# Last tile's layer-2 rows transposed on TensorE, the w1 jobs' normalised rows loaded behind the last w2 loads, and three VectorE costs in the planner

## The chip, the cores and the metric

The kernel runs on one core of a Trainium2 chip. The metric is device time in microseconds (us) of one execution, the median of three runs. The core's engines run side by side, each through a list of instructions fixed when the kernel is built: TensorE (PE, with its weight loads shown apart as PEld), VectorE (DVE), ScalarE (ACT), GpSimd (POOL) and SyncE (SP). In this kernel SP and POOL mostly issue DMA transfers; the profile shows the issuing of a transfer as SPq or ACTq.

## The reference

The reference is the forward and backward pass of four residual layers over x, 2048 rows of 448 in bf16: a convolution layer A, a dense layer B, then A and B again with the same weights.

```python
def _A_ref(q, k, v, shift_k, ssm_k, ssm_D):    # q is the normalised x
    k_shift = ...                              # 4-tap shift of k along the sequence
    kv = k_shift * v
    y = irfft(rfft(kv, 2S) * rfft(ssm_k, 2S))[:S] + kv * ssm_D
    return q * y

def _B_ref(x, w1, w2):                         # w1 448x1792, w2 1792x448
    return silu(x @ w1) @ w2

x = A_q
x = x + _A_ref(_layernorm(x), A_k, A_v, A_shift_k, A_ssm_k, A_ssm_D)
x = x + _B_ref(_layernorm(x), B_w1, B_w2)
x = x + _A_ref(_layernorm(x), A_k, A_v, A_shift_k, A_ssm_k, A_ssm_D)
x = x + _B_ref(_layernorm(x), B_w1, B_w2)
```

It returns x and the gradients of all eight inputs for a given `grad_out`; those of w1 and w2 are sums over all 2048 rows and over both dense layers.

## The kernel before

The kernel has four stages. `Head` computes the convolution y through FFTs written as matmuls. `Flow.tile(j)` then takes the 16 tiles of 128 rows through both dense layers forward and back, software-pipelined over the tiles. `Tail` ends with the gradient of the convolution (`fft`, in 14 chunks of 1024 columns, then `loads` and `ends`) and with the weight gradients (`jobs("w2")`, `jobs("w1")`).

No order is written out. Every piece of work is an operation `s.op(cost, fn, r, w, prio, ...)`: the cost in us on each engine that may take it, the tiles it reads and writes, and a priority (lower is more urgent, mostly a due time). `Sched.plan` (from L257) plays these through with the given costs and with rates for the transfers, and fixes from that on which engine each runs and in which order; `Sched.emit` writes the instructions out in that order. On the chip an engine follows its list, and an instruction starts when the data and buffers that it needs are there. The argument `after=` ties an operation to others in the plan, and `behind=` says that it may be planned only when the others have been issued; neither is itself a wait on the chip. A cost is thus never executed: it moves work only through the plan.

What the change and the steps of the prediction touch:

- `ON_PE` (L595) lists the (tile, kind) pairs whose rows are transposed by four TensorE matmuls (`ps_t`, L645) and a copy out of PSUM (`nT`). All others are transposed by two DMA transposes on SP (`nT`, L636 and L637). Kind 0 is the first dense layer's input, 1 the second's, 2 the backward pass of the first. `Flow.turn` does this.
- The second dense layer of tile j: its normalised rows `n3` go through `turn` to the matmuls `ps_h` (L663), and ScalarE makes `aT` and `dT` from them (L700). The stores of these rows are DMA transposes into `turned` (L717) followed by `A_d<-turned` (L718); `GH_d<-ghT` (L711) stores the backward rows.
- For the last tile a part of `aT` is also transposed into `lastA` (L792). The gradient rows `gmov` (four transfers, L1087) are planned behind it.
- `jobs(which)` makes 7 jobs of 256 weight columns each. A job has two groups of 2 x 16 matmuls `ps_d` (L1169) of 128x448, which read a block `jb` of stored rows, 1 MB, and the matching other operand: for w2 `gmov` with the rows A1 and `G2` (`G` in the profile) with the rows A0; for w1 `nmov`, the normalised rows of the second layer with GH1 and of the first layer with GH0. `bring` loads the blocks on SP: plain copies `jb<-A_d` for w2 (L1114), DMA transposes `jb<-GH_d` for w1 (L1112). The blocks share three buffers, and for w1 a fourth, so a load waits until the block three places earlier is used up. `k.load` chains these loads by `behind=`.
- Before the change the first w2 block is planned behind the last tile's second DMA transpose (`self.last_rows`), and the four `nmov` loads (L1095, two for each of the layers, 896 KB each) are planned by priority alone.
- The chunks (`Tail.chunk`): two matmuls `ps_s` (L904) make the transform, a copy takes it to `xx_c`, two VectorE copies swap its halves (L912, L913), two VectorE products make `pq` (L918), 16 matmuls each turn these into `ps_v` (L924, L925), and copies take them to `B1k` and `Zg`. The copies out of PSUM can go to ScalarE or VectorE, as the planner sees fit. `ps_s`, `ps_v`, `ps_gkv` and `ps_gK` share three PSUM buffers.
- After the chunks come `ps_gkv` (L980), `ps_gK` (L1002), `ps_gD` (L1014) and `ps_sk` (L1051). The planner spreads the w2 jobs' matmuls between all of these as fillers.

Of the kernel before, what the change touches and what calls it, by code (L numbers as in the profile page):

```python
# [14 lines left out]
ACT = mybir.ActivationFunctionType  # L15
ALU = mybir.AluOpType
# [4 lines left out]
P = 128  # L21
# [68 lines left out]
def _copy(nc, eng, out, in_):  # L90
    if eng is nc.scalar:
        nc.scalar.copy(out, in_)  # L92
    else:
        eng.tensor_copy(out, in_)  # L94
# [38 lines left out]
class Sched:  # L133
# [26 lines left out]
    def at(self, base, *key):  # L160
        return base + NUDGE.get(key, 0.0)
# [188 lines left out]
def _pm(ap2d):  # L350
    return ap2d.rearrange("(p j) d -> p j d", j=J)
# [240 lines left out]
NT1 = {1: "nTG", 2: "nT3", 3: "nT3"}  # L592
COPIED = (0, 2,)
RAW = ("GH0", "GH1")
ON_PE = ((0, 0), (0, 1), (1, 0), (2, 0), (3, 0), (4, 0), (14, 2), (15, 0), (15, 2))  # L595


class Flow:
# [162 lines left out]
    def tile(self, j):  # L761
        nc, s, k = self.nc, self.s, self.k
        b = T_ * j
        at = lambda kind, base: s.at(base, j, kind)
# [11 lines left out]
        s.op({"POOL": 0.6}, lambda e: nc.gpsimd.dma_start(out=_pm(k.N_d[0][:])[:, j, :], in_=n1[:]), r=[n1], w=[k.st_[("n", 0, j)]], prio=b + 10, dma=("plain", 115e3))  # L776
        a1, s1 = self.silu(self.turn(n1, at("t1", b - 3), NT1.get(j, "nT1"), (j, 0) in ON_PE), 0, at("h1", b), (j, 0) in TURNED, j in COPIED)
        self.store(a1, "A0", j, b + 4)
# [7 lines left out]
        c = b + T_ + SKEW[0]  # L786
        a2, s2 = self.silu(self.turn(n3, at("t3", c + 2.7), "nT3", (j, 1) in ON_PE), 1, at("h2", c + 5.6), (j, 1) not in TURNED)
        up2 = self.last_up
        k.load = [] if (j, 1) in ON_PE else [self.last_rows]
        if j == NT - 1:  # L790
            k.lastA = s.vb("J", "lastA", [P, 4, P], BF16, "lastA")
            k.lastA_op = s.op({"SP": 1.2}, lambda e: nc.sync.dma_start_transpose(out=k.lastA[:], in_=a2[:, 0:4, :].rearrange("p a s -> p (a s)")), r=[a2], w=[k.lastA], prio=c + 10, dma=("turn", 131e3))  # L792
# [19 lines left out]
        d = c + T_ + SKEW[1]  # L812
        gh1 = self.grad_up(self.turn(G2, at("tG", d + 14), "nTG", (j, 2) in ON_PE), s1, at("gG", d + 16.9))
        self.store(gh1, "GH0", j, d + 20)
# [24 lines left out]
class Tail:  # L839
# [53 lines left out]
    def chunk(self, ci, Z, z, pr):  # L893
        nc, s, k = self.nc, self.s, self.k
        lo = 1024 * ci
        sp = self.sp[ci % 3]
        for i, nm in enumerate(("KV", "K")):
            s.op({"POOL": 0.6}, lambda e, i=i, nm=nm: nc.gpsimd.dma_start(out=sp[i][:], in_=k.SPEC_d[nm][:, lo:lo + 1024]), r=[k.spd[nm, ci // 2]], w=[sp[i]], prio=pr - 20, after=self.s1 if ci < 3 else (), dma=("plain", 262e3))
        ps = self.unit([P, 1024], name="ps_s2")

        def mm(e):
            zf = Z[:].rearrange("q a b -> q (a b)")
            for h in range(2):
                nc.tensor.matmul(ps[:, 512 * h:512 * h + 512], lhsT=k.Gsb[:, G_FWD, :], rhs=zf[:, lo + 512 * h:lo + 512 * h + 512], start=True, stop=True)  # L904

        o = s.op({"PE": 0.44}, mm, r=[z], w=[ps], prio=pr, after=[o for x in self.xx[ci % 3][1:] for o in x.readers])
        self.marks.append(o)
        xx, xa, xh = self.xx[ci % 3]
        s.op({"ACT": 1.02, "DVE": 1.15}, lambda e: _copy(nc, e, xa[:], ps[:]), r=[ps], w=[xa], prio=pr)

        def swap(e):
            nc.vector.tensor_copy(xh[0:64, :], xa[64:128, :])  # L912
            nc.vector.tensor_copy(xh[64:128, :], xa[0:64, :])  # L913

        s.op({"DVE": 0.75}, swap, r=[xa], w=[xh], prio=pr)
        for i, (B1, cnd) in enumerate(((self.B1k, True), (z, False))):
            pq = s.vb("P1", "pq", [P, 2, 1024], BF16, "pq")
            s.op({"DVE": 1.15}, lambda e, i=i, pq=pq: nc.vector.tensor_tensor(out=pq[:], in0=xx(), in1=sp[i][:].unsqueeze(1).to_broadcast([P, 2, 1024]), op=ALU.mult),  # L918
                 r=[xa, xh, sp[i]], w=[pq], prio=pr)
            pv = self.unit([P, 8, P], name="ps_v")  # L920

            def inv(e, pq=pq, pv=pv):
                for m in range(8):
                    nc.tensor.matmul(pv[:, m, :], lhsT=pq[:, 0, m * P:(m + 1) * P], rhs=k.Gsb[:, G_IAC, :], start=True, stop=False)  # L924
                    nc.tensor.matmul(pv[:, m, :], lhsT=pq[:, 1, m * P:(m + 1) * P], rhs=k.Gsb[:, G_IBC, :], start=False, stop=True)  # L925

            s.op({"PE": 0.92}, inv, r=[pq], w=[pv], prio=pr)

            def out(e, pv=pv, B1=B1, cnd=cnd):
                if cnd:  # L930
                    _copy(nc, e, B1[:, :, 32 * ci:32 * ci + 32].rearrange("p q (dh ds) -> p dh q ds", ds=4), pv[:].rearrange("p dh (q ds) -> p dh q ds", ds=4))
                else:
                    _copy(nc, e, Z[:, 8 * ci:8 * ci + 8, :].rearrange("p a b -> p (a b)"), pv[:].rearrange("p a b -> p (a b)"))

            s.op({"ACT": 1.03, "DVE": 1.17}, out, r=[pv], w=[B1], prio=pr)

    def loads(self, pr):
        nc, s, k = self.nc, self.s, self.k
# [143 lines left out]
    def jobs(self, which, pr):  # L1082
        nc, s, k = self.nc, self.s, self.k
        if which == "w2":
            gm = s.vb("res", "W1", [P, NT, D], BF16, "gmov")
            gs = [gm.sub() for _ in range(4)]
            gl = [lambda i=i: s.op({"SP": 0.4}, lambda e: nc.sync.dma_start(out=gm[:, 4 * i:4 * i + 4, :], in_=_pm(k.grad_out[0])[:, 4 * i:4 * i + 4, :]), w=[gs[i]], prio=pr - 30, dma=("plain", 458e3), behind=[k.lastA_op]) for i in range(4)]  # L1087
            groups = [("A1", [gs[t // 4] for t in range(NT)], lambda t: gm[:, t, :]), ("A0", k.G2v, lambda t: k.G2[:, t, :])]
        else:
            nm = [s.vb("PF", ("A1", "B1v")[i], [P, NT, D], BF16, "nmov") for i in range(2)]  # L1090
            nh = [[v.sub() for _ in range(2)] for v in nm]
            for i in (1, 0):
                for h in range(2):
                    hs = slice(8 * h, 8 * h + 8)
                    s.op({"SP": 0.4}, lambda e, i=i, hs=hs: nc.sync.dma_start(out=nm[i][:, hs, :], in_=_pm(k.N_d[i][:])[:, hs, :]),  # L1095
                         r=[k.st_[("n", i, j)] for j in range(8 * h, 8 * h + 8)], w=[nh[i][h]], after=self.done[i], prio=pr - 30 if i else pr + 0.5, dma=("plain", 917e3))
            groups = [("GH1", [nh[1][t // 8] for t in range(NT)], lambda t: nm[1][:, t, :]), ("GH0", [nh[0][t // 8] for t in range(NT)], lambda t: nm[0][:, t, :])]
        out7 = k.outs[7].rearrange("(c p) f -> p c f", p=DC)
        prev = []
# [2 lines left out]
        def fetch(p, gi, spare=False):  # L1102
            if (p, gi) not in have:
                have[p, gi] = (s.vb(*(("PF", "Minv") if spare else ("J", "jb")), [P, NT, 256], BF16, "jb"), [None] * NT, spare)
            return have[p, gi]

        def bring(p, gi, lo, hi, at=None):
            b, part, spare = fetch(p, gi, which == "w1" and (2 * p + gi) % 4 == 0)
            nm = groups[gi][0]
            src, n, fs = k.rows_d[nm], hi - lo, slice(256 * p, 256 * p + 256)  # L1110
            if nm in RAW:
                cost, kind, get = 0.3 * n, "load", lambda e: nc.sync.dma_start_transpose(out=b[:, lo:hi, :], in_=src[fs, P * lo:P * hi])  # L1112
            else:
                cost, kind, get = 0.4, "plain", lambda e: nc.sync.dma_start(out=b[:, lo:hi, :], in_=src[:, lo:hi, fs])  # L1114
            v = b.sub()
            part[lo:hi] = [v] * (hi - lo)
            k.load = [s.op({"SP": cost}, get,
                 r=[k.st_[(nm, j)] for j in range(lo, hi)], w=[v], prio=pr + 12.5 * p + gi if at is None else at, dma=(kind, 65e3 * n), behind=k.load, after=self.done[0] if spare else ())]

        if which == "w2":  # L1120
            bring(0, 1, 0, 16)
            for x in gl:
                x()
            for a in ((0, 0, 0, 15), (1, 1, 0, 16), (1, 0, 0, 15)):
                bring(*a)
        else:
            for p, gi, at in ((0, 0, pr), (1, 0, pr + 0.2), (0, 1, pr + 1), (1, 1, pr + 2)):
                bring(p, gi, 0, 16, at)
# [243 lines left out]
```

## Time and profile before

| what | value |
|---|---|
| median of 3 runs | 708.87 us (708.34 to 709.3) |
| the profiled execution's time | 712.63 us |
| its span (first to last instruction) | 710.8 us |
| PE busy | 682.0 us, 96% |
| DVE busy | 514.7 us, 72% |
| ACT busy | 407.1 us, 57% |
| POOL busy | 152.9 us, 22% |
| matmuls `ps_d` of `jobs`, nmov, gmov and G | 87.6 + 45.9 + 45.2 us busy |
| DMA moved | 150.64 MB, 212 GB/s on the mean |

The timeline of an engine lists its instructions in order, merged where equal ones follow each other: start, duration, engine, line, operation, tiles, shape, count, and in brackets the idle time before it and what ended that. Matmuls overlap in such rows, so the pace of a group is read from its start to the start of the next. A row of SPq is the issuing of a transfer, not its running; "DMA to landing" is counted from the start of the issue to the arrival. The view of waits gives who waited for whom: us in total, times, longest.

### The profile page before, as it was taken

To read this page: it belongs to the slowest core of one execution; us is meant where nothing else is said; L and a number is where in the kernel's file an instruction comes from. 1 tells how busy PE (TensorE), PEld (TensorE's weight loads), DVE (VectorE), ACT (ScalarE), POOL (GpSimd) and SP (SyncE) were. 2 spreads that over 40 slices of the span, in tenths; PEclk is the share of its full clock that TensorE was granted. 3 is DMA by queue.
4 is the path that set the end of the run, shared out by engine and by line. 5 is a ranking of instruction groups with operands and counts; after the bars stand their busy time and mean duration, and the time that the engine had idled before them with its cause. 6 is when DMAs were issued, how large, how long until landed. Compare 5 with 4: busy or idle time off the path is not lost. (4 is left out here: it accounts for less than half of the span.)

```text
span 710.8 us, 18075 instructions
## 1 busy us (share of the span) xinstructions
PE 682.0 (96%) x7490; PEld 473.5 (67%) x7508; DVE 514.7 (72%) x1205; ACT 407.1 (57%) x495; POOL 152.9 (22%) x266
## 2 busy tenths in 40 slices
PE   6999889999999999999999999799999999999996
PEld 5887657777676777677776776555667754555553
DVE  5989798578888888888888887634699758665000
ACT  4989986786667765676656855215876550011321
POOL 1154153103222232222222100021142131100000
PEclk9999999999999999999999999999999999999999
DMA  9979989879788879887888679957599599999771
GB/s 330 277 249 290 350 168 176 189 180 199 165 180 167 178 186 201 195 152 174 175 189 171 144 167 276 281 148 236 200 357 321 163 339 306 246 218 207 173 127 28
DMA packets 277504, 150.64 MB, mean 212 GB/s; under 512 B 224878, under 2 KB 258846, under 8 KB 277036
## 3 DMA queue, kind: packets, MB, share of 16 engines
q1 hardware_dynamic: 263646, 108.42, 64.7%
q0 software_dynamic: 13008, 40.24, 18.7%
q8 instruction: 59, 0.97, 0.6%
q10 hardware_dynamic: 766, 0.80, 0.5%
q14 instruction: 25, 0.20, 0.1%
HBM read 50.68 MB, written 54.60 MB: 148 GB/s over the span
## 5 line engine op out<-in xcount | busy, mean ns | idle before, releaser
L1169 PEld LDWEIGHTS <-jb 128*128 128x128 bf16 x892 | 85.5, 98 | 82.8 <-issue 4.3
L92 ACT CAST ghp<-ps_g 128x896 bf16<-128x896 f32 x64 | 58.1, 908 | 64.9 <-PE ps_g L672 54.9
L726 PE MATMUL ps_o<-w2sb,aT 128*128 128x448 bf16 x448 | 89.7, 352 | 0.8 <-ACT aT L700 0.8
L726 PE MATMUL ps_n<-w1T,ghT 128*128 128x448 bf16 x448 | 90.0, 352 | 0.0
L1169 PE MATMUL ps_d<-nmov,jb 128*128 128x448 bf16 x448 | 87.6, 353 | 0.0
L663 PE MATMUL ps_g<-nT,w2T 128*128 128x128 bf16 x1344 | 86.8, 221 | 0.0
L663 PE MATMUL ps_h<-nT,w1sb 128*128 128x128 bf16 x1344 | 85.6, 219 | 0.8 <-ACT nT L92 0.8
L663 PEld LDWEIGHTS <-w2T 128*128 128x128 bf16 x1344 | 78.4, 99 | 7.6 <-issue 0.4
L663 PEld LDWEIGHTS <-w1sb 128*128 128x128 bf16 x1344 | 76.7, 98 | 5.2 <-issue 0.9
L726 PEld LDWEIGHTS <-aT 128*128 128x128 bf16 x448 | 43.0, 98 | 38.4 <-ACT aT L700 1.0
L726 PEld LDWEIGHTS <-ghT 128*128 128x128 bf16 x448 | 43.1, 98 | 37.8
L700 ACT ACTIVATE aT<-ps_h 128x896 bf16<-128x896 f32 x64 | 56.7, 916 | 19.9 <-PE ps_h L672 11.0
L622 POOL TENSOR_TENSOR rstd<-ve,mhalf 128x1 f32<-128x1 f32 x64 | 39.3, 614 | 106.8 <-DVE ve L619 106.7
L700 ACT ACTIVATE dT<-ps_h 128x896 bf16<-128x896 f32 x60 | 53.3, 915 | 14.9 <-PE ps_h L672 10.0
L750 DVE SCALAR_TENSOR_TENSOR junk<-u,n 128x448 bf16<-128x448 bf16 x64 | 39.9, 624 | 25.5 <-ACT u L829 24.4
L1169 PE MATMUL ps_d<-gmov,jb 128*128 128x448 bf16 x220 | 45.9, 354 | 5.9 <-DMA gmov<-in_grad_out_dram 4.1
L700 ACT ACT_TABLE_LOAD x36 | 46.2, 1283 | 1.2 <-issue 0.6
L1169 PE MATMUL ps_d<-G,jb 128*128 128x448 bf16 x224 | 45.2, 353 | 0.1
L739 DVE TENSOR_TENSOR ghT<-ghp,dT 128x896 bf16<-128x896 bf16 x64 | 39.4, 620 | 5.5 <-ACT ghp L92 5.5
L92 ACT CAST dob<-ps_d 128x448 bf16<-128x448 f32 x14 | 7.5, 532 | 60.6 <-PE ps_d L1169 60.6
L617 DVE BATCH_NORM_STATS2 st<-x 128x6 f32<-128x448 bf16 x64 | 40.0, 625 | 1.5
L829 ACT ACTIVATE u<-ps_n,rstd 128x448 bf16<-128x448 f32 x32 | 20.3, 636 | 33.2 <-POOL rstd L622 13.8
(178 smaller groups left out, 1217.6 us busy)
## 6 DMA issues: line engine op xcount, KB each, us to landing
A_d<-turned SPq DMA_DIRECT2D x32, 448.0 KB, 4.2
GH_d<-ghT SPq DMA_DIRECT2D x32, 448.0 KB, 4.3
jb<-A_d SPq DMA_DIRECT2D x12, 1024.0 KB, 9.0
KK<-KK POOLq DMA_DIRECT2D x14, 256.0 KB, 5.0
spec_K<-KK POOLq DMA_DIRECT2D x7, 512.0 KB, 5.5
spec_KV<-X POOLq DMA_DIRECT2D x7, 512.0 KB, 8.2
N_d<-n POOLq DMA_DIRECT2D x32, 112.0 KB, 3.3
sp_c<-spec_KV POOLq DMA_DIRECT2D x14, 256.0 KB, 6.1
```

The source lines that it names most:

```text
L92: nc.scalar.copy(out, in_)
L617: nc.vector.bn_stats(out=st[:], in_=x[:])
L622: s.op({"POOL": 1.0}, lambda e: nc.gpsimd.tensor_tensor(out=rs[:], in0=ve[:], in1=self.k.mhalf[:, 0:1], op=ALU.pow), r=[ve], w=[rs], prio=pr)
L663: nc.tensor.matmul(ps[:, i, :], lhsT=at(b, ft), rhs=nT[:, b, :], **f)
L700: prev = [s.op({"ACT": 0.93}, lambda e, i=i, fun=fun, out=out, late=late: nc.scalar.activation(out[:, 7 * i:7 * i + 7, :], c[:, 7 * i:7 * ...
L726: nc.tensor.matmul(po[:, :D], lhsT=a[:, ft, :], rhs=wt[:, ft * D:(ft + 1) * D], start=(ft == 0), stop=(ft == NF - 1))
L739: s.op({"DVE": 0.57}, lambda e, i=i, t=t: nc.vector.tensor_tensor(out=gh[:, 7 * i:7 * i + 7, :], in0=t[:], in1=d[:, 7 * i:7 * i + 7, :], o ...
L750: nc.vector.scalar_tensor_tensor(out=junk[:], in0=u[:], scalar=1.0, in1=n[:], op0=ALU.mult, op1=ALU.mult, accum_out=cp[:, 1:2])
L829: s.op({"ACT": 0.85}, lambda e: nc.scalar.activation(u[:], pn[:, :D], ACT.Identity, scale=r[:], accum_out=cp[:, 0:1]), r=[pn, r], w=[u, cp ...
L1169: nc.tensor.matmul(ps[:, :D], lhsT=rows(t, gi, u), rhs=at(t), start=(first and t == ts[0]), stop=(last and t == ts[-1]))
```

## The change

Three edits. The pair (15, 1), the last tile's second layer, joins `ON_PE`: two DMA transposes go from SP, four TensorE transposes and one copy out of PSUM are added, and the first w2 block is no longer planned behind the DMA transposes. `bring` keeps all its loads in `k.loads`, and the second layer's two `nmov` loads are planned behind the last but one load of w2, the first layer's two behind the last one. Three costs of VectorE in the chunks change: the swap from 0.75 to 0.86, the product from 1.15 to 1.23, the copy out of `ps_v` from 1.17 to 1.24 us.

```diff
-ON_PE = ((0, 0), (0, 1), (1, 0), (2, 0), (3, 0), (4, 0), (14, 2), (15, 0), (15, 2))
+ON_PE = ((0, 0), (0, 1), (1, 0), (2, 0), (3, 0), (4, 0), (14, 2), (15, 0), (15, 1), (15, 2))
...
-        k.load = [] if (j, 1) in ON_PE else [self.last_rows]
+        k.loads, k.load = [], [] if (j, 1) in ON_PE else [self.last_rows]
...
-        s.op({"DVE": 0.75}, swap, r=[xa], w=[xh], prio=pr)
+        s.op({"DVE": 0.86}, swap, r=[xa], w=[xh], prio=pr)
...
-            s.op({"DVE": 1.15}, lambda e, i=i, pq=pq: nc.vector.tensor_tensor(...
+            s.op({"DVE": 1.23}, lambda e, i=i, pq=pq: nc.vector.tensor_tensor(...
...
-            s.op({"ACT": 1.03, "DVE": 1.17}, out, r=[pv], w=[B1], prio=pr)
+            s.op({"ACT": 1.03, "DVE": 1.24}, out, r=[pv], w=[B1], prio=pr)
...
-                         r=[...], w=[nh[i][h]], after=self.done[i], prio=pr - 30 if i else pr + 0.5, dma=("plain", 917e3))
+                         r=[...], w=[nh[i][h]], after=self.done[i], prio=pr - 30 if i else pr + 0.5, dma=("plain", 917e3), behind=k.loads[-1 - i:][:1])
...
-            k.load = [s.op({"SP": cost}, get,
-                 ..., behind=k.load, after=self.done[0] if spare else ())]
+            k.loads.append(s.op({"SP": cost}, get,
+                 ..., behind=k.load, after=self.done[0] if spare else ()))
+            k.load = k.loads[-1:]
```

The order that the planner builds is the same in both kernels up to the last tile's second layer, on every engine, and differs from there on. On SP the first block `jb<-A_d` follows `turned` at once, the second is moved ahead of one `GH_d` store, and the end of the w2 loads reads: the last but one block, the second layer's `nmov` twice, the last block, one `jb<-GH_d`, the first layer's `nmov` twice, then the other `jb<-GH_d` (before: the four `nmov`, the last but one block, the last block, all `jb<-GH_d`). On TensorE, before the last tile's backward matmuls, the row `G` 15, `ps_n` 14, `gmov` 5, `ps_t` 4, `gmov` 5, `ps_g` 56, `gmov` 15 (matmuls) becomes `G` 10, `ps_n` 14, `G` 5, `ps_t` 4, `gmov` 5, `ps_g` 56, `gmov` 15. In the chunks VectorE keeps two copies to `B1k` and two to `xx_c`, where it had four to `B1k`, two to `xx_c` and one to `Zg`; ScalarE takes the three. Between the last `ps_gK` and `ps_gD` stand 8 matmuls of `G`, one unit of `ps_gkv` and 8 of `G`, where there were 8 of `G`.

More of the change, by code (lines that the diff above doesn't have):

```diff
@@ L913, in swap @@
             nc.vector.tensor_copy(xh[64:128, :], xa[0:64, :])
-        s.op({"DVE": 0.75}, swap, r=[xa], w=[xh], prio=pr)
+        s.op({"DVE": 0.86}, swap, r=[xa], w=[xh], prio=pr)
         for i, (B1, cnd) in enumerate(((self.B1k, True), (z, False))):
             pq = s.vb("P1", "pq", [P, 2, 1024], BF16, "pq")
-            s.op({"DVE": 1.15}, lambda e, i=i, pq=pq: nc.vector.tensor_tensor(out=pq[:], in0=xx(), in1=sp[i][:].unsqueeze(1).to_broadcast([P, 2, 1024]), op=ALU.mult),
+            s.op({"DVE": 1.23}, lambda e, i=i, pq=pq: nc.vector.tensor_tensor(out=pq[:], in0=xx(), in1=sp[i][:].unsqueeze(1).to_broadcast([P, 2, 1024]), op=ALU.mult),
                  r=[xa, xh, sp[i]], w=[pq], prio=pr)
@@ L1095, in jobs @@
                     s.op({"SP": 0.4}, lambda e, i=i, hs=hs: nc.sync.dma_start(out=nm[i][:, hs, :], in_=_pm(k.N_d[i][:])[:, hs, :]),
-                         r=[k.st_[("n", i, j)] for j in range(8 * h, 8 * h + 8)], w=[nh[i][h]], after=self.done[i], prio=pr - 30 if i else pr + 0.5, dma=("plain", 917e3))
+                         r=[k.st_[("n", i, j)] for j in range(8 * h, 8 * h + 8)], w=[nh[i][h]], after=self.done[i], prio=pr - 30 if i else pr + 0.5, dma=("plain", 917e3), behind=k.loads[-1 - i:][:1])
             groups = [("GH1", [nh[1][t // 8] for t in range(NT)], lambda t: nm[1][:, t, :]), ("GH0", [nh[0][t // 8] for t in range(NT)], lambda t: nm[0][:, t, :])]
@@ L1116, in bring @@
             part[lo:hi] = [v] * (hi - lo)
-            k.load = [s.op({"SP": cost}, get,
-                 r=[k.st_[(nm, j)] for j in range(lo, hi)], w=[v], prio=pr + 12.5 * p + gi if at is None else at, dma=(kind, 65e3 * n), behind=k.load, after=self.done[0] if spare else ())]
+            k.loads.append(s.op({"SP": cost}, get,
+                 r=[k.st_[(nm, j)] for j in range(lo, hi)], w=[v], prio=pr + 12.5 * p + gi if at is None else at, dma=(kind, 65e3 * n), behind=k.load, after=self.done[0] if spare else ()))
+            k.load = k.loads[-1:]
         if which == "w2":
```

## The prediction

> **What bounds the kernel now.** First the page's totals: which engine has no room.
>
> ```profile
> span 710.8 us, 18075 instructions
> PE 682.0 (96%) x7490; PEld 473.5 (67%) x7508; DVE 514.7 (72%) x1205; ACT 407.1 (57%) x495; POOL 152.9 (22%) x266
> ```
>
> TensorE works 682.0 of 710.8 us. The change takes no matmul away, so it can only win in the 28.8 us in which TensorE stands idle, and it loses wherever it opens a new gap. So the second view is TensorE's own waits, all over the span, of which these four lie where the two kernels differ and are above half a us.
>
> ```profile
> PE ps_d L1169 <- DMA gmov<-in_grad_out_dram: 4.1, 3, 2.5
> PE ps_v L924 <- DVE pq L918: 2.2, 4, 0.9
> ...
> PE ps_d L1169 <- DMA jb<-A_d: 1.7, 1, 1.7
> ...
> PE ps_gD L1014 <- DVE gKD L1008: 0.8, 1, 0.8
> ```
>
> They come to 8.8 us: the last tile's rows of `gmov`, the chunks' `pq`, one w2 block, and `ps_gD` after the chunks. Each edit has one of the first three in its reach. I take them in order of time.
>
> **The last tile's transposes and the loads behind them.** TensorE at the end of the tiles, then SP there, then ScalarE's last `aT`:
>
> ```profile
> 447.51 3.00 PE L1169 MATMUL ps_d<-G,jb 128*128 128x448 bf16 x15
> 450.35 2.81 PE L726 MATMUL ps_n<-w1T,ghT 128*128 128x448 bf16 x14
> 454.52 0.92 PE L1169 MATMUL ps_d<-gmov,jb 128*128 128x448 bf16 x4 [1.36 <-DMA gmov<-in_grad_out_dram]
> 455.68 0.35 PE L1169 MATMUL ps_d<-gmov,jb 128*128 128x448 bf16 x1 [0.24 <-DMA gmov<-in_grad_out_dram]
> 455.87 0.38 PE L645 MATMUL ps_t<-ident,G 128*128 128x128 bf16 x4
> 456.09 0.73 PE L1169 MATMUL ps_d<-gmov,jb 128*128 128x448 bf16 x3
> 459.30 0.90 PE L1169 MATMUL ps_d<-gmov,jb 128*128 128x448 bf16 x2 [2.48 <-DMA gmov<-in_grad_out_dram]
> ```
>
> ```profile
> 418.95 3.62 SPq L717 DMA_TRANSPOSE turned<-aT  x1
> 422.66 1.22 SPq L636 DMA_TRANSPOSE nT<-n  x1
> 423.93 1.23 SPq L637 DMA_TRANSPOSE nT<-n  x1
> 425.20 0.59 SPq L1114 DMA_DIRECT2D jb<-A_d  x1
> ...
> 436.98 5.46 SPq L792 DMA_TRANSPOSE lastA<-aT  x1
> ```
>
> ```profile
> 435.88 1.73 ACT L700 ACTIVATE aT<-ps_h 128x896 bf16<-128x896 f32 x2
> ```
>
> Price of the added transposes: four take 456.09 - 455.87 = 0.22 us of TensorE before the next group starts. The copy into `nT` falls to ScalarE between two pairs of `ghp` copies and is needed only a whole `ps_g` and a `ps_n` later, about 5.6 us; without that cover it would add its 0.6 us once. What it takes from SP is 1.22 + 1.23 us of issuing and the transfers behind it.
>
> *Where a page says otherwise: the Trainium skill, "TensorE: Matmul & The Clock Gate", Part 4 (PE-mode transpose), gives about 390 ns for one transpose of this size alone and about 275 ns in a kernel. By that the four would cost an estimated 1.1 to 1.6 us and the sum below would come out at 703.7 to 704.2. The trace disagrees: the step of 0.22 us for four is above, and I keep it.*
>
> Now the order. Let everything be 0.22 us late and let TensorE never wait; a `ps_d` or `ps_n` matmul takes (450.35 - 447.51) / 15 = 0.189 us, one of the 56 of a `ps_g` group at most the 0.22 / 4 of a transpose, 3.1 for the group. Then `G` x10 runs from 447.73, `ps_n` from 449.62, `G` x5 from 452.27, `ps_t` from 453.22, the five `gmov` from 453.44, `ps_g` from 454.39 and the next `gmov` from 457.5. Between the second and the third part of `gmov` there is now a whole `ps_g`. The idle times above end at the landings: first part 454.52, second 455.68, third 459.30. If they land no earlier than before, the waits are 454.52 - 453.44 = 1.08, then for the fifth matmul 455.68 - (454.52 + 0.76) = 0.40, and none for the third, wanted after three more matmuls, at 457.5 + 1.48 + 0.57 = 459.55. So the order alone brings 4.08 down to 1.48. How much earlier can they land? The first block moves from 425.20 to the end of `turned`, 422.57, so 1 MB starts 2.6 us sooner; but `lastA`, ahead of `gmov` on SP, waits for `aT`, which ends at 437.61 + 0.22 whatever SP does, and one `GH_d` store moves behind the second block. Between 0 and 2.6 us earlier, then; half of it covers the 1.08 us. I leave 0.3 us of waiting: **3.8 us won here**, bounds 1.5 (`ps_g` or `ps_n` waits 1 us for its operand) and 4.1, minus 0.22 of the transposes.
>
> **The chunks.** VectorE and ScalarE in the chunk stage, and the engines' sums over it:
>
> ```profile
> L918 DVE TENSOR_TENSOR pq<-xx_c,sp_c 128x2048 bf16<-128x2048 bf16 x28 | 33.1, 1221 | 0.6
> L912 DVE COPY xx_c<-xx_c 64x1024 bf16<-64x1024 bf16 x14 | 5.9, 422 | 0.4
> L913 DVE COPY xx_c<-xx_c 64x1024 bf16<-64x1024 bf16 x14 | 5.9, 421 | 0.2
> L94 DVE CAST B1k<-ps_v 128x1024 bf16<-128x1024 f32 x4 | 4.9, 1223 | 0.5 <-PE ps_v L925 0.4
> ```
>
> ```profile
> L92 ACT CAST Zg<-ps_v 128x1024 bf16<-128x1024 f32 x13 | 13.2, 1014 | 6.7 <-PE ps_v L925 6.5
> ```
>
> ```profile
> 504.57:561.28 56.71, 54.13 (x592) 39.11 (x597) 52.98 (x63) 37.97 (x40) 15.42 (x25) 1.00 0.93 311
> ```
>
> The columns after the length are PE, PEld, DVE, ACT and POOL busy, the clock, the DMA share and GB/s. TensorE has 54.1 and VectorE 53.0 us of work in 56.7: two engines nearly level, so VectorE is late at times and the four `pq` waits follow. The old costs had the planner believe VectorE faster than these rows (1.15 for 1.22, 0.75 for two copies of 0.42). With the new ones three copies of 1.22 us leave it: 53.0 - 3.7 = 49.3. ScalarE takes 3 x 1.01, 38.0 + 3.0 = 41.0, and has room. Does TensorE still wait? A chunk costs VectorE 0.84 + 2 x 1.22 = 3.3 us. A chunk without a filler of eight `ps_d` costs TensorE only the 32 `ps_v` and a transform, 2.2 us by their pace, one with a filler 3.7. In the new order the third and the sixth chunk have none; there VectorE falls 1.1 us behind, of which the chunks before have saved up a part. I leave 0.9 of 2.2: **1.3 us won**, bounds: 2.2 won, or 1.3 lost if ScalarE, with three jobs of 1.01 us a chunk, delays the three shared PSUM buffers (0.25 us a chunk x 14 = 3.5 us of waits).
>
> **After the chunks.** The `ps_gD` wait should go, since 8 matmuls of `G`, a unit of `ps_gkv` (four such matmuls) and 8 of `G` stand before it, 20 x 0.189 = 3.8 us, where there were 8, 1.5. The order of the `ps_gK` and `ps_gkv` around it is new too, and for that I give back 0.3: **0.5 won**, bounds 0.8 won and 1.6 lost (a wait of the old one's kind at each of the three later `gK` outputs, 3 x 0.8 = 2.4, in place of one).
>
> **The `nmov` loads.** SP and TensorE around the last w2 blocks, then how the `nmov`, the first of the two blocks, an earlier undisturbed block and the `GH_d` loads land and issue:
>
> ```profile
> 576.64 4.29 SPq L1095 DMA_DIRECT2D nmov<-N_d  x4
> 584.26 11.06 SPq L1114 DMA_DIRECT2D jb<-A_d  x2
> ```
>
> ```profile
> 584.06 6.22 PE L1169 MATMUL ps_d<-gmov,jb 128*128 128x448 bf16 x32
> ...
> 599.38 6.23 PE L1169 MATMUL ps_d<-gmov,jb 128*128 128x448 bf16 x32 [1.72 <-DMA jb<-A_d]
> ```
>
> ```profile
> L1095 SPq DMA_DIRECT2D nmov<-N_d x4: 320/433/1462, 576.6 to 580.4; - x4
> ...
> DMA to landing us min/median/max: 9.7/12.7/15.0
> ```
>
> ```profile
> DMA to landing us min/median/max: 15.1/15.1/15.1
> ```
>
> ```profile
> DMA to landing us min/median/max: 8.3/8.3/8.3
> ```
>
> ```profile
> L1112 SPq DMA_TRANSPOSE jb<-GH_d x5: 4587/4842/9852, 595.5 to 621.5; - x5
> ```
>
> Before, the last but one block is issued at 584.26 behind four `nmov` and needs 15.1 us; an earlier one, with no `nmov` about, needed 8.3. TensorE was ready for it at 599.38 - 1.72 = 597.66, 13.6 us after it began the job before: 64 matmuls, 12.1, and two `ps_sk` of 0.75. With `nmov` behind it, it is there in time: **1.7 won**. But the first layer's two `nmov` now stand ahead of the second `jb<-GH_d`, and all of them start 8 us later. Count from T, the start of job 5 (584.06 before). SP's transfers land one after another: `nmov` every (580.4 + 15.0 - 576.6 - 9.7) / 3 = 3.0 us, a block 4.0 after it (584.26 + 15.1 - 595.4), a `GH_d` every 4.8. Then the last but one block lands at T + 8.3, `nmov` at 14.3, the last block at 18.3, `GH_d` at 23.1, `nmov` at 29.1, the next `GH_d` at 33.9 and 38.7. By the new order (32 matmuls are 6.05 us, and a `ps_sk` falls in each half job but one) TensorE wants them at T + 13.6, 27.2, 20.4, 27.2, 40.0, 33.2 and 40.0. Only the second `GH_d` is late, by 0.7; since the 8.3 comes from a quieter stretch I take **1.0 us, set against the gain**; bounds 0 and 11 (below).
>
> The sum: 3.8 + 1.3 + 0.5 + 1.7 - 0.2 - 1.0 = 6.1 us. The profiled execution took 712.63, 1.8 more than its span and 3.8 more than the median of 708.87; all terms are idle stretches of fixed work, so I take the same 6.1 from the median: **702.8 us**.
>
> **The rivals.** *The loads land no earlier.* For it: `aT` sets `lastA`. Against: 2.6 us of SP's time and a full queue move up. It leaves 1.5 instead of 0.3: 704.0.
>
> *The chunks only move their waits.* ScalarE is already at 38.0 of 56.7 us and gets more; against: its copies were waiting for `ps_v` (6.5 us of idle before `Zg`). With 3.5 us of waits instead of 0.9: 705.4.
>
> *The plan deals the gaps out anew.* The planner's transfers have fixed rates, the trace's landings vary from 8.3 to 15.1 us, so another block can be the late one: all of 6.1 goes back, 708.9. Against: each named wait has its cause removed, not moved.
>
> *The `GH_d` loads starve the w1 jobs (slower).* Place: from the last but one block on. If that block takes 15.1 us even without `nmov` (the outputs on POOL's queue are still there) and each `GH_d` 6.5 (26 us for the four issues from 595.5 to 621.5), the landings are T + 15.1, 21.1, 25.1, 31.6, 37.6, 44.1: TensorE waits 1.5 for the first, 3.2 for the last block and 6.2 for the second `GH_d`, 10.9 in all instead of 1.0: 712.7. For it: TensorE uses a block in 6.05 us, so no time lost is made up; against: 8.3 without `nmov`. Above 7.1 us of waits here the change loses, above 8.5 visibly.
>
> **How the numbers follow.** 0.2%, or 1.4 us, is about what a measurement of this kernel can tell from no change. Chances: the forecast 0.59, loads no earlier 0.11, chunks 0.10, gaps anew 0.07, starved 0.13. The first three are faster: 0.80; the fourth same: 0.07; the last slower: 0.13. The forecast's own range is 700.0 (its waits all vanish, none comes: 4.1 + 2.2 + 0.8 + 1.7 - 0.2 = 8.6, 700.3, and a little below for the waits under half a us) to 706; for 8 in 10 the upper end goes to 709.0, past the fourth case.
>
> **What would show it.** Right: no `gmov` wait above 1 us before the last `ps_g`; VectorE near 49 us in the chunk stage and `pq` waits under 1.5; the last but one block landing in 8 to 11 us, no wait for `jb<-A_d`; at most a small one for `jb<-GH_d`. Wrong: a `jb<-GH_d` or `nmov` wait above 4 us, TensorE waiting for ScalarE's copies in the chunks, or 1 us and more around the added `ps_t`.

## The result, and the profile after

The changed kernel takes 704.90 us, the median of 8 runs (703.73 to 708.28), against 708.87 (708.09 to 710.4, 8 runs) for the kernel before on the same chip: a ratio of 0.9944 with a 95% interval of 0.9926 to 0.9961. That is 3.97 us faster, where 6.1 were forecast; the forecast time was 702.8 and its range 700.0 to 709.0.

The two profiled executions differ by more, 712.63 - 703.73 = 8.90 us. The one of before was 712.63 - 708.87 = 3.76 slower than its kernel's median, the one of after 704.90 - 703.73 = 1.17 faster than its own; 8.90 - 3.76 - 1.17 = 3.97. The totals of the page after:

```profile
span 701.9 us, 18099 instructions
PE 681.8 (97%) x7512; PEld 472.8 (67%) x7512; DVE 513.5 (73%) x1204; ACT 408.2 (58%) x497; POOL 152.4 (22%) x266
```

TensorE's work is the same 682 us; what went is idle time. TensorE's waits of the kernel after (total us, times, longest), those that lie where the kernels differ:

```profile
PE ps_d L1170 <- DMA jb<-GH_d: 1.4, 1, 1.4
...
PE ps_dt L1191 <- ACT dob L92: 1.1, 2, 0.7
...
PE ps_v L924 <- DVE pq L918: 0.3, 1, 0.3
```

The `gmov` wait, the `ps_gD` wait and the `jb<-A_d` wait have no row any more, and `pq` is down from 2.2 to 0.3. New are 1.4 us at `jb<-GH_d`, and at `dob` 1.1 instead of the 0.5 us that before had there. TensorE's timeline at the end of the tiles (start, us, instruction, count; a bracket would show idle time):

```profile
447.95 2.06 PE L1170 MATMUL ps_d<-G,jb 128*128 128x448 bf16 x10
449.84 2.81 PE L726 MATMUL ps_n<-w1T,ghT 128*128 128x448 bf16 x14
...
453.47 0.38 PE L645 MATMUL ps_t<-ident,G 128*128 128x128 bf16 x4
453.69 1.11 PE L1170 MATMUL ps_d<-gmov,jb 128*128 128x448 bf16 x5
...
457.58 3.00 PE L1170 MATMUL ps_d<-gmov,jb 128*128 128x448 bf16 x15
```

No row there has a bracket, and each start lies 0.1 to 0.25 us behind the one worked out in the prediction. The first three parts of `gmov` land at 452.28, 454.13 and 456.69 us (454.48, 455.64 and 459.26 in the profile of before), each ahead of its first use. The chunk stage, from the first `ps_s` to the first `ps_gK` (length, then PE, PEld, DVE, ACT and POOL busy):

```profile
497.51:552.32 54.81, 54.42 (x600) 39.26 (x598) 49.59 (x60) 39.26 (x42) 15.42 (x25) 1.00 0.89 301
```

VectorE has 49.6 us of work there instead of 53.0, and TensorE is busy for all but 0.4 us. Then SP's queue around the last w2 blocks and the `nmov` loads, and TensorE where it waits:

```profile
575.27 0.52 SPq L1114 DMA_DIRECT2D jb<-A_d  x1
576.02 2.39 SPq L1095 DMA_DIRECT2D nmov<-N_d  x2
581.99 0.52 SPq L1114 DMA_DIRECT2D jb<-A_d  x1
582.69 11.39 SPq L1112 DMA_TRANSPOSE jb<-GH_d  x1
594.17 1.01 SPq L1095 DMA_DIRECT2D nmov<-N_d  x2
595.27 26.78 SPq L1112 DMA_TRANSPOSE jb<-GH_d  x4
```

```profile
597.40 4.71 PE L1170 MATMUL ps_d<-G,jb 128*128 128x448 bf16 x24
601.95 6.22 PE L1170 MATMUL ps_d<-nmov,jb 128*128 128x448 bf16 x32
609.59 1.69 PE L1170 MATMUL ps_d<-nmov,jb 128*128 128x448 bf16 x8 [1.43 <-DMA jb<-GH_d]
...
628.65 0.43 PE L1191 MATMUL ps_dt<-ident,dob 128*112 128x128 bf16 x4 [0.68 <-ACT dob L92]
```

The second `GH_d` block is issued at 595.27, right behind the first layer's two `nmov`, and TensorE gets it at 609.59. The view of that one load gives its time:

```profile
L1112 SPq DMA_TRANSPOSE jb<-GH_d x1: 10434/10434/10434, 595.3 to 595.3; - x1
...
DMA to landing us min/median/max: 14.3/14.3/14.3
```

### The profile page after: what moved, and what is told of

It reads as the page before. It is cut to its first block, busy times and chain, and to the rows that moved or that the text cites. A ratio compares the mean times of both kernels' runs of the same rounds, so it can differ in the third digit from the quotient of the medians.

```text
span 701.9 us, 18099 instructions
## 1 busy us (share of the span) xinstructions
PE 681.8 (97%) x7512; PEld 472.8 (67%) x7512; DVE 513.5 (73%) x1204; ACT 408.2 (58%) x497; POOL 152.4 (22%) x266
## 5 line engine op out<-in xcount | busy, mean ns | idle before, releaser
L622 POOL TENSOR_TENSOR rstd<-ve,mhalf 128x1 f32<-128x1 f32 x64 | 39.3, 614 | 106.8 <-DVE ve L619 106.7
```

The source lines that it names most:

```text
L622: s.op({"POOL": 1.0}, lambda e: nc.gpsimd.tensor_tensor(out=rs[:], in0=ve[:], in1=self.k.mhalf[:, 0:1], op=ALU.pow), r=[ve], w=[rs], prio=pr)
```

## The experiments

The change has three edits: P (the last tile's pair in `ON_PE`), N (the `nmov` loads behind the w2 loads) and C (the three VectorE costs). All their combinations were timed, each ratio against the kernel before in the same comparison:

```
edits   median us (runs)   ratio to before [95%]
before  708.87 (8); in the later comparisons 709.35 (28), 708.96 (17), 709.99 (19)
P       707.63 (11)        0.9960 [0.9940, 0.9979]
N       712.73 (12)        1.0051 [1.0025, 1.0077]
C       711.64 (12)        1.0018 [0.9992, 1.0045]
P N     706.70 (12)        0.9956 [0.9933, 0.9979]
P C     703.20 (6)         0.9909 [0.9874, 0.9944]
        702.90 (6)         0.9886 [0.9851, 0.9921]
N C     716.78 (6)         1.0108 [1.0063, 1.0153]
P N C   704.90 (8)         0.9944 [0.9926, 0.9961]   (the changed kernel)
        705.39 (8)         0.9928 [0.9901, 0.9954]
```

### The kernel before, once more

No edit: a second profiled execution, to see which of the waits belong to the kernel and which to the execution.

> The kernel before, unchanged, once more. Theory A: the profiled execution of before (712.63 us) was a slow one among its own, and its waits on landings (gmov 4.1, the w2 block 1.7) are larger than usual. Then this one takes about 709 us and the four named waits (8.8 us) come to 4 to 6. Rival: a profile of this kernel always has these waits and costs some 3.8 us over a timed run; then about 712.5 us and 8.8 us again.

It took 707.26 us. Its waits, same columns:

```profile
PE ps_v L924 <- DVE pq L918: 2.2, 4, 0.9
PE ps_d L1169 <- DMA gmov<-in_grad_out_dram: 2.1, 3, 1.3
...
PE ps_d L1169 <- DMA jb<-A_d: 0.2, 1, 0.2
```

The `pq` waits are the same to a tenth; what waits for a DMA is not: `gmov` 2.1 instead of 4.1, `jb<-A_d` 0.2 instead of 1.7. With `ps_gD`, 1.3 instead of 0.8, the four waits on which the prediction rests are 5.9 us here instead of 8.8, so the first theory holds. And there is a second difference. Windows of the first profile of before around the last `gmov` wait (the eighth column is the granted TensorE clock, behind the five engines):

```profile
455.64:459.05 3.41, 1.14 (x8) 0.61 (x8) 3.17 (x11) 0.59 (x1) 0.00 (x0) 1.00 0.95 285
459.05:462.46 3.41, 3.16 (x26) 2.51 (x27) 0.52 (x2) 0.00 (x0) 0.54 (x1) 0.50 0.94 275
```

TensorE was busy for 1.14 of 3.41 us, and for the next 3.41 us its clock was 0.50. The same stretch of the second profile:

```profile
459.05:462.46 3.41, 3.41 (x29) 2.07 (x27) 1.25 (x2) 1.33 (x2) 0.04 (x1) 1.00 0.32 86
```

There it was 1.00. So the `gmov` waits had cost 1.6 us more, half of the 3.16 us that TensorE worked at that clock, which no row of waits shows: the work behind a wait ran at half speed.

### P alone

```diff
-ON_PE = (..., (14, 2), (15, 0), (15, 2))
+ON_PE = (..., (14, 2), (15, 0), (15, 1), (15, 2))
```

> Only the pair (15, 1) in ON_PE, with the load chain that follows from it. Theory A (each edit takes away its own wait): no gmov wait before the last ps_g, added ps_t at 0.22 us; the pq waits near 2 us and a wait for the w2 block stay; 1.5 to 3 us under before, about 706.5. Rival B (the gain is the new costs' plan alone): the gmov wait goes but comes back at a later load, within 0.7 us of before.

Measured: 0.9960, 1.7 us. The waits and the windows around the longest:

```profile
PE ps_v L924 <- DVE pq L918: 2.2, 4, 0.9
PE ps_d L1169 <- DMA jb<-A_d: 1.9, 1, 1.9
```

```profile
589.58:592.99 3.41, 1.52 (x38) 0.79 (x37) 2.33 (x4) 0.53 (x1) 1.28 (x2) 1.00 1.15 312
592.99:596.41 3.42, 3.42 (x11) 1.42 (x10) 0.00 (x0) 0.00 (x0) 0.00 (x0) 0.50 1.22 241
```

The `gmov` wait is gone, the `pq` waits stand. TensorE comes to the last-but-one w2 block earlier, the block doesn't, so a part goes back at `jb<-A_d`: 1.9 us, and 1.7 more by the half clock behind it.

### N alone

```diff
-  ... prio=pr - 30 if i else pr + 0.5, dma=("plain", 917e3))
+  ... prio=pr - 30 if i else pr + 0.5, dma=("plain", 917e3), behind=k.loads[-1 - i:][:1])
```

> Only the nmov loads planned behind the last w2 blocks. Theory A: the gmov and pq waits stay as before, the wait for jb<-A_d goes (1.7 in the profile), a wait for jb<-GH_d of about 1.4 us comes; 0 to 1.5 us under before, about 708. Rival: the second jb<-GH_d is later than in the changed kernel and this edit alone loses 1 us or more.

Measured: 1.0051, slower. The waits of its profile:

```profile
PE ps_d L1170 <- DMA gmov<-in_grad_out_dram: 2.2, 3, 1.3
...
PE ps_d L1170 <- DMA jb<-GH_d: 1.3, 1, 1.3
...
PE ps_dt L1191 <- ACT dob L92: 1.1, 2, 0.7
```

The wait at `jb<-A_d` is gone, 0.2 us in the second profile of before, and 1.3 came at `jb<-GH_d` and 0.7 at `dob`: the waits are those of the first theory, the time is not. The rival had the loss, but not its reason, since the second `GH_d` block takes 14.2 us here and 14.3 in the changed kernel. The profiled execution took 710.89 and had no stretch of half clock; of the 12 runs, the five with a mean granted clock of 0.998 or more took 709.42 to 711.93, the seven below 712.02 to 719.24. Where those seven lost their clock, no trace shows.

### C alone

```diff
-        s.op({"DVE": 0.75}, swap, ...)
+        s.op({"DVE": 0.86}, swap, ...)
-            s.op({"DVE": 1.15}, lambda e, i=i, pq=pq: nc.vector.tensor_tensor(...
+            s.op({"DVE": 1.23}, lambda e, i=i, pq=pq: nc.vector.tensor_tensor(...
-            s.op({"ACT": 1.03, "DVE": 1.17}, out, ...)
+            s.op({"ACT": 1.03, "DVE": 1.24}, out, ...)
```

> Only the three VectorE costs. Theory A: the pq waits fall from 2.2 to under 0.7 us, VectorE's copies out of PSUM in the chunks from 7 to about 4; the other waits stay; 1 to 2 us under before, about 707.4. Rival B (this edit carries the gain): 3 us or more under before.

Measured: 1.0018, an interval that holds 1. TensorE's waits, then SP's wait ahead of the `nmov` loads, then the windows:

```profile
PE ps_d L1169 <- DMA jb<-A_d: 4.6, 1, 4.6
...
PE ps_v L924 <- DVE pq L918: 0.3, 1, 0.3
```

```profile
SPq L1095 <- PE ps_gK L1002: 18.8, 1, 18.8
```

```profile
590.48:593.89 3.41, 0.09 (x1) 0.10 (x2) 3.41 (x6) 0.00 (x0) 0.85 (x2) 1.00 1.21 290
593.89:597.30 3.41, 3.41 (x10) 1.34 (x10) 3.38 (x5) 0.00 (x0) 0.54 (x1) 0.50 1.34 316
```

The chunks win 1.9 us as the first theory has it, which left out that `jb<-A_d` takes it back: the `nmov` loads, ahead of that block on SP, wait for `ps_gK` to free their space. TensorE stands 4.6 us, and then runs 3.4 us at half speed.

### Two edits at a time

Each is the changed kernel without one edit (the diffs above, undone). First without C:

> The changed kernel without the new VectorE costs. Theory A, each edit takes away the waits of its own place: the traces of the single edits show the gmov waits gone with the ON_PE pair (2.1 us in the second profile of before) and the last-but-one w2 block's wait gone with the later nmov loads, at the price of about 1.3 us at jb<-GH_d and 0.7 us at dob; what stays against the changed kernel is the pq waits, 2.2 us in every trace with the old costs and 0.3 us with the new. So 1.5 to 2.5 us over the changed kernel: ratio to before 0.996 to 0.998, no gmov and no jb<-A_d wait, pq waits of 2.2 us. Theory B, the edits' single effects add (pair ON_PE 0.9960, later nmov 1.0051): ratio 1.001.

Then without N:

> The changed kernel with the nmov loads left where they were. Theory A: pq waits of about 0.5 us, no gmov wait, but the chunk stage ends 2 us earlier and the last-but-one w2 block, which still lands behind the four nmov loads, doesn't: the wait at jb<-A_d comes to 2 to 5 us (4.6 with the new costs alone, 1.9 with the ON_PE pair alone), while the 1.4 us at jb<-GH_d and 0.7 us at dob of the changed kernel go. Ratio to before 0.996 to 1.000. Theory B, the single effects add (0.9960 and 1.0018): 0.998, with a jb<-A_d wait no longer than the 1.9 us that the ON_PE pair alone showed.

And without P:

> The changed kernel without the ON_PE pair, so the last tile's h2 is turned by DMA as before. Theory A: the gmov waits stay, 1.5 to 4 us, pq waits of about 0.5 us, no jb<-A_d wait, 1.3 us at jb<-GH_d; 2 to 4 us over the changed kernel, ratio 0.997 to 1.000. Theory B, the single effects add (1.0051 and 1.0018): ratio 1.007, that is 5 us slower than before.

Without C: 706.70, 0.9956. The `pq` waits were 1.7, not 2.2, and `jb<-GH_d` 1.7; the rest is as the first theory has it. Without N: 703.20, faster than the changed kernel. Its wait at that block, SP's wait and the second `GH_d` load:

```profile
PE ps_d L1169 <- DMA jb<-A_d: 0.6, 1, 0.6
```

```profile
SPq L1095 <- PE ps_gK L1002: 10.1, 1, 10.1
```

```profile
L1112 SPq DMA_TRANSPOSE jb<-GH_d x1: 4290/4290/4290, 598.0 to 598.0; - x1
...
DMA to landing us min/median/max: 7.1/7.1/7.1
```

Both theories missed the time here, and the first the wait too. With P the space of the `nmov` loads comes free earlier (they start at 570.52, with C alone at 574.48), so the block behind them is 0.6 us late and not 2 to 5; no half clock follows; and the second `GH_d` block lands 7.1 us after its issue, half of what it takes in the changed kernel.

Without P: 716.78, 1.0108, the slowest of all. Its waits, and the windows around the longest:

```profile
PE ps_d L1170 <- DMA jb<-GH_d: 4.4, 1, 4.4
PE ps_d L1170 <- DMA gmov<-in_grad_out_dram: 1.9, 1, 1.9
```

```profile
610.97:614.39 3.42, 0.36 (x2) 0.00 (x0) 0.00 (x0) 0.00 (x0) 0.00 (x0) 1.00 1.21 255
614.39:621.22 6.83, 5.45 (x15) 2.19 (x16) 0.00 (x0) 0.00 (x0) 0.00 (x0) 0.50 1.17 252
```

Here the half clock lasted 6.83 us, in which TensorE worked for 5.45: another 2.7 lost. The second theory's 1.007 lies in the interval here, the first theory's 0.997 to 1.000 does not. In the two cases before, the sum of the single effects lies outside the measured interval (1.001 against 0.9956, and 0.998 against 0.9909), so in general the edits' gains don't add. That each takes away just the waits of its own place is only half the truth, since N also adds one, which is 1.3 to 1.9 us long in four profiles and 4.4 here.

### The changed kernel and P C side by side

> The changed kernel once more, beside the others of this call. Theory C, the later nmov loads cost more than they bring: about 1.4 us of wait at the second jb<-GH_d and 0.7 us at dob in every execution, so 705 us and 1.5 to 2.5 us more than the kernel with the ON_PE pair and the new costs alone. Theory D, the 1.7 us between these two in separate comparisons (704.9 and 703.2) were the chip's noise: the same time within 0.5 us.

> The ON_PE pair and the new costs, nmov loads as before, for a comparison with the changed kernel on one chip. Theory C: 703 us, 1.5 to 2.5 us under the changed kernel; at jb<-A_d a wait under 1.5 us, no wait at jb<-GH_d, the second GH_d block landing about 7 us after its issue. Theory D: 705 us like the changed kernel. If its jb<-A_d wait comes out over 1.9 us, the granted clock falls to half for 3.4 us behind it, and it would be 704 to 707.

705.39 (703.86 to 707.12) against 702.90 (701.18 to 704.04) on one chip. N costs about 2.5 us in the company of P and C. In profiles it is 1.4 to 1.9 us at `jb<-GH_d` and 0.7 at `dob`, against 0.6 to 0.8 at `jb<-A_d` in the two profiles of P C.

### The first layer's nmov loads further back

The changed kernel with these two loads behind the second `GH_d` block, and then behind the third, where the condition reads `(p, gi) == (0, 1)`; `rows_in` is the old loop's body as a function:

```diff
-  for i in (1, 0): ... behind=k.loads[-1 - i:][:1]
+  rows_in(1, k.loads[-2:][:1])
...
+  if (p, gi) == (1, 0):
+      rows_in(0, k.loads[-1:])
```

> The changed kernel with the first layer's two nmov loads planned behind the second jb<-GH_d block instead of ahead of it. Theory C1, those two loads on SP's queue are what makes the second GH_d block late (14.3 us from issue to landing in the changed kernel, 7.1 without them ahead): it lands near 602 us of the span, seven us ahead of its use, the 1.4 us wait goes, none takes its place: 702 to 703.5 us, level with or under the kernel without the later nmov loads. Theory C2, the transposing loads are slow whatever stands between them: the wait moves to the third GH_d block or to nmov, over 1 us there, and the time stays at 704.5 to 706.

> The same with the two loads behind the third jb<-GH_d block. Theory C1: as the one before, 702 to 703.5 us, no wait at jb<-GH_d; if the first layer's rows then land after their first use, a wait at ps_d<-nmov of 1 to 4 us and 704 to 707. Theory C2: a wait over 1 us at the fourth GH_d block, 704.5 to 706.

Behind the second block: 708.17 us, slower than the changed kernel. Its SP queue, the third `GH_d` load, and the windows around TensorE's wait for it:

```profile
582.75 16.94 SPq L1114 DMA_TRANSPOSE jb<-GH_d  x2
599.78 1.01 SPq L1095 DMA_DIRECT2D nmov<-N_d  x2
600.89 23.27 SPq L1114 DMA_TRANSPOSE jb<-GH_d  x3
```

```profile
L1114 SPq DMA_TRANSPOSE jb<-GH_d x1: 12539/12539/12539, 600.9 to 600.9; - x1
...
  PE ps_d L1174: 3.7, 1
...
DMA to landing us min/median/max: 17.7/17.7/17.7
```

```profile
616.26:619.67 3.41, 1.00 (x6) 0.54 (x7) 0.00 (x0) 0.00 (x0) 0.00 (x0) 1.00 1.28 188
619.67:623.08 3.41, 3.41 (x40) 1.58 (x39) 1.10 (x4) 0.00 (x0) 0.00 (x0) 0.50 1.09 237
```

The second block was in time; the third, now behind the pair, took 17.7 us, and TensorE stood 3.7 us for it. The wait moved to the third block, as the second theory said, though the time it named was too low. Behind the third block: 702.29 us (701.71 to 703.38), ratio 0.9885 [0.9854, 0.9915]. The fourth block, now behind the pair:

```profile
L1114 SPq DMA_TRANSPOSE jb<-GH_d x1: 8926/8926/8926, 606.4 to 606.4; - x1
...
DMA to landing us min/median/max: 13.3/13.3/13.3
```

It takes its 13.3 us too, but TensorE wants it later, and no wait for any `GH_d` block is left. So both theories hold a part: a `GH_d` load right behind the two `nmov` is slow, 13.3 to 17.7 us wherever it stands, and whether that costs anything is a matter of the block it hits. This kernel and P C beat the changed one; between the two, 702.29 and 702.90, the runs don't tell.

### The account

For each profiled execution, from the first `ps_h` to the end of TensorE's work; idle time of TensorE there, from 400 us on; and half of the time that TensorE worked at half clock (worked out from the traces):

```
kernel           stretch    idle   half clock   rest
before            612.70   10.31         1.58   600.8
before again      608.33    7.39            -   600.9
P                 607.31    5.07         1.71   600.5
N                 609.55    8.37            -   601.2
C                 611.07    9.13         1.71   600.2
P N               606.55    4.86            -   601.7
P C               602.15    1.57            -   600.6
P C again         602.32    1.73            -   600.6
N C               612.50    9.06         2.73   600.7
P N C             603.89    3.07            -   600.8
P N C again       604.36    3.53            -   600.8
pair behind 2nd   607.54    5.25         1.71   600.6
pair behind 3rd   602.31    1.65            -   600.7
```

The rest is the same within 1.5 us in all of them, and within 1.0 in twelve of thirteen: idle time and half clock explain the differences. The first `ps_h` itself starts between 91.9 and 94.4 us, whatever the kernel. These 2.5 us go with the moment at which the granted clock first rises to full speed: 10.2 and 10.4 us after the start in the two profiles in which `ps_h` starts at 91.9 and 92.0, and 15.3 to 17.8 us in the others, with `ps_h` at 93.0 to 94.4. The kernels have the same order up to there, so the edits have no part in it.

## Why the prediction was right, and where it was not

The side and the range were right, and most of the mechanism. The gain is 2.1 us under the forecast, and two steps made that.

*Point by point.*

- The last tile's transposes: 0.22 us forecast for the four; 453.69 - 453.47 = 0.22 in the profile after. The 1.1 to 1.6 us by the figure of the Trainium skill, "TensorE: Matmul & The Clock Gate", Part 4, did not come. The `gmov` waits were to leave 0.3 us; they left nothing. The first part landed 2.2 us earlier than in the profile the forecast was read from, within its bounds of 0 to 2.6, so the rival that the loads land no earlier is out.
- The chunks: 49.3 us of VectorE forecast, 49.6 measured; `pq` waits of 0.9 forecast, 0.3 measured. ScalarE had 39.3 us of work, not 41.0, and no wait of TensorE there ended on it. The term was 1.3, the profiles show 1.9.
- After the chunks: 0.5 forecast; the waits at `ps_gD` and `ps_gK` both went, 0.8 + 0.5. Both are gone with P alone too; C alone and N C have no wait at `ps_gD`, but 1.3 us at `ps_gK` instead of 0.5. So this part of the gain belongs to the order that comes with P.
- The `nmov` loads: with T = 575.07 in the profile after, the second `GH_d` block was to be wanted at T + 33.2 and land at T + 33.9. It was wanted at 609.59 - 1.43 = 608.16, T + 33.1, and landed 14.3 us after 595.27, T + 34.5: 1.4 us of waiting against the 1.0 set down. The rival that the `GH_d` loads starve named this place; its 10.9 us of waits did not come, since the last-but-one block landed at T + 6.6 (6.4 us after its issue at 575.27) and not at T + 15.1.

*What failed.* First, the size of the terms: the prediction said that "all terms are idle stretches of fixed work, so I take the same 6.1 from the median". They are not fixed. The two terms that end on a DMA, `gmov` and `jb<-A_d`, were 4.1 + 1.7 us in the execution it read, 2.1 + 0.2 in the next one, and the 3.8 us by which that execution lay over the median were a sign of it. The sum with the waits of the second profile of before is 2.1 + 0.2 at the two DMA terms, 1.9 at `pq` and 1.8 at `ps_gD` and `ps_gK`, less 1.4 at `jb<-GH_d`, 0.6 at `dob` and 0.2 for the transposes: 3.8 us, against 3.97 measured. So the forecast came as near as it did partly by luck: its DMA terms were 3.2 us too large and its engine terms, 1.3 + 0.5, were 1.9 too small. The part that half clock takes was missing too: 1.6 us in the profile of before, where the mean clock was 0.996. It adds to what that one execution had to lose, and explains nothing of the 2.1.

Second, the edit of the `nmov` loads was taken as 1.7 - 1.0 = 0.7 us won. Beside the other two edits it loses about 2.5 (705.39 against 702.90 on one chip; 1.7 in separate comparisons, 704.90 against 703.20). What it removes is 0.6 to 0.8 us, since with P and C the `nmov` loads get their space earlier and the block behind them is hardly late; what it adds is 1.4 to 1.9 at `jb<-GH_d` and 0.7 at `dob`. The last was not in the prediction: in the new order a `ps_dt` follows at once the `ps_d` group whose `dob` it reads, where the kernel without the edit has a `ps_sk` of about 0.6 us between them, and TensorE waits for ScalarE's cast. That the plan deals the waits out anew, a rival with 0.07, is what C, N C and the pair behind the second block show; in the changed kernel it took a part of the gain.

*Where a wait costs more than itself.* The granted clock is 1.00 or 0.50 in all traces, the changes from one to the other stand 3.41 us apart or a multiple of it, and it fell behind waits of 1.9 (P), 2.5 (before), 3.7 (pair behind the second block), 4.4 (N C) and 4.6 us (C); it didn't behind the 1.4 of the changed kernel, the 1.7 of P N, the 1.7 at `jb<-A_d` in before or the 1.9 at `gmov` in N C. Nor did it, in any of the traces, behind the 1.8 or 1.9 us near 106 us of the span in which the `ps_t` of an early tile waits for VectorE's `n`. The Trainium skill, "TensorE: Matmul & The Clock Gate", Part 1 (The HAM clock gate), has the same two states, a free-running window of about 3.4 us, and the return to half speed after at least one idle window. The traces agree on the window and the states; an idle window was not needed: P lost the clock behind one in which TensorE worked for 1.52 of 3.41 us.

## What to carry to other kernels

Before a wait of one profiled execution goes into a sum, take a second profile of the same kernel: here the waits on a DMA (4.1 and 2.1 us, 1.7 and 0.2) differed far more than those on an engine (2.2 and 2.2, 0.8 and 1.3). A TensorE wait of some 2 us or more may cost up to another 1.7 us of half clock, 2.7 in the one case where that lasted 6.83 us. And where several edits go into one plan, leave each out of the whole in turn rather than measure it alone: alone, C showed nothing, since it brought a wait of 4.6 us, and beside P it is worth 4 to 5 us (707.63 against 703.20 and 702.90, in separate comparisons), of which `pq` is 1.9 and a shorter wait at `jb<-A_d`, with no half clock behind it, 1.3 + 1.7; N takes the wait of 4.6 us away and costs 2.5 us beside the other two.

## What the runs showed of the hardware that was not expected

A DMA-transposed 1 MB load (`GH_d`) that stands right behind plain loads on SP holds the queue while it is issued: 8.9, 10.4, 11.4 and 12.5 us in the rows above, 4.3 where another `GH_d` load was ahead of it. Behind the two `nmov` it took 13.3 to 17.7 us from issue to landing, against 7.1 there, and the queue stands for whatever is planned behind it. The traces show what the hold goes with: of the 182 `GH_d` loads in the thirteen, none ends its issue before the transfer ahead of it on SP has landed; it ends 0.7 to 6.6 us after that. In the changed kernel the second `nmov` lands at 604.35 and the issue ends at 605.70. The plain load issued at 581.99, with an `nmov` ahead of it in flight until 587.17, took 0.52 us all the same. Behind the `out_dram` stores later in the w1 jobs, which land at most 3.8 us after the `GH_d` issue begins, that issue takes 3.9 to 6.4 us. So the issue goes with how long the transfer ahead is still under way, and not with that one being plain. This is read from the order of events; no run tested it by itself.

All changes of the granted clock in one execution lie on one grid of 3.41 us steps that starts with the first rise to full speed (15.75 us after the start in the profile after, 10.21 in that of C). So it matters for a wait of 1.9 us whether it falls into one step of the grid: P's did, while the 1.9 us at `jb<-GH_d` in the second profile of the changed kernel and the 1.9 at `gmov` in N C, each cut by a boundary of its grid, did not. That alone does not decide it. The 1.86 us wait of the `ps_t` in the profile after lies in one step, 104.49 to 107.90, and the clock stayed at 1.00 behind it:

```profile
104.49:107.90 3.41, 1.55 (x9) 0.64 (x8) 3.24 (x11) 2.46 (x3) 1.30 (x3) 1.00 1.09 252
```

A step with 1.55 us of work kept the clock, P's with 1.52 lost it. Whether the work in a step is what decides, and whether the line lies there, is open: the two differ by 0.03 us, and where a matmul ends is modelled in the traces.

Not tried were the second layer's `nmov` loads moved alone, and a cover for the 0.7 us at `dob`.
